# First batch of an attention kernel: scores by products of 64 rows, products with the values by 64 columns

## The chip, the core and the metric

The kernel runs on one NeuronCore of a Trainium2 chip. Its engines work side by side and wait for each other through semaphores: TensorE (PE) does matrix products and transposes, VectorE (DVE), ScalarE (ACT) and GpSimd (POOL) work element by element, SyncE (SP) issues most transfers. The metric is the device time of one execution in microseconds; lower is better.

## The reference

Three layers follow one another. Only the first is touched, and of it only the first of four batches.

```python
# q, k, v: 4 batches, 8 heads, 576 positions, head size 64
scores = scale * np.matmul(q, k.transpose(0, 1, 3, 2))
thresh = np.max(scores, axis=-1, keepdims=True) - tau
scores = np.where(scores >= thresh, scores, -1000000000.0)
attn = np.exp(scores - np.max(scores, axis=-1, keepdims=True))
attn = attn / (np.sum(attn, axis=-1, keepdims=True) + 1e-09)
x = np.matmul(attn, v)            # then 2304 tokens x 512
g = s * np.maximum(x @ w_in, 0) ** 2 + b
x = g @ w_out                     # d_ff 2048
h = x @ w_in2
out = (np.maximum(h, 0) + alpha * np.minimum(h, 0)) @ w_out2
```

## The kernel before

The instruction order is not written by hand. Every step is a task given to a planner (`Plan`, lines 114 to 216) with the engine that may do it, an assumed cost, the buffers it reads and writes, and a rank. `Plan.run` simulates the engines with these costs and emits, for each free engine, the ready task of lowest rank. A changed cost or a changed buffer thus changes the order of everything around it. `pe(n, k)` (line 244) is the assumed cost of `k` passes over `n` columns.

Attention works on pairs of heads: `pair(p)` (line 605), p = 0 to 3 for the first batch, 4 to 15 for the rest. A tile has 128 rows, so a pair's two heads of size 64 fill it. A pair has nine score tiles: four of each head (128 queries each) and one that holds the last 64 queries of both heads (`i == NQ`). The first batch is special (`first`, `whole`, `PLAIN`): its products are done in full f32, where each product appears in the trace as two weight loads and two matmul records. Later batches split every operand into a high and a low fp32r part (`hk`, `hq`, `gh`, `gl`) and are not touched here.

For a pair of the first batch:

- `transpose` (line 658, issued from line 660) turns k and q so that the head's dimensions lie on the rows. Evictions follow: L668 copies all 576 columns of k into `k32` in two instructions, and L676 (DVE) or L678 (ACT) writes q into `q32`, once for each head, multiplied by `sc_h[h]`, which holds the scale in that head's 64 rows and zero in the other 64.
- `score` (line 737, issued from L742) multiplies one 128x128 block of `q32` with `k32` in two products of 288 keys each, one for each half of the keys, into the two halves of a `sc` buffer. All 128 rows take part, the zeros in `q32` cancel the other head. There are two `sc` buffers.
- L752 (DVE) takes the negated maximum, L756 (ACT) the exponential, L758 (DVE) the threshold and the row sums. Each reads all of the `sc` buffer.
- `group` (line 838) turns a head's exponentials by 128 keys at a time (L877, and L881 for the shared tile), L887 (ACT) copies them into `gf` or `sh`, and `product` (line 845, issued from L852) multiplies them with the values. The weights of this product are `vt.t[:, c]`: the values of both heads, 128 columns, of which the 64 of the other head are of no use. 256 queries (`gi` 0) or 320 (`gi` 1) stream through; five products, one for each block of keys, add up in one bank. There are two heads and two `gi` for each pair: 16 groups, 80 products.
- `finish` (line 927) copies the bank into `z` (L934, ACT): for head 1 first over all 128 rows, then for head 0 over its 64 rows.

While this goes on, the planner fits in the preparation of the first weights (L351 to L411) and, once tokens and weights are there, the products of the second layer (L480 to L482, block A: the first 1536 tokens over part of the hidden size), whose rank is far behind all of attention. When all of attention is done, `switch` (line 1012) frees its memory and the rest of the two layers follows.

Of the kernel before, what the change touches and what calls it, by code (L numbers as in the profile page):

```python
# [12 lines left out]
AF = mybir.ActivationFunctionType  # L13
# [4 lines left out]
P = 128  # L18
# [201 lines left out]
def tile_kernel(ctx: ExitStack, tc: tile.TileContext, q, k, v, tau, w1i, w1o, s_in, b_in, w2i, w2o, alpha, out):  # L220
# [53 lines left out]
    def tiles(pool, n, name, shape, dt=F32):  # L274
        return [pool.tile(shape, dt, name=f"{name}{i}") for i in range(n)]
# [282 lines left out]
    def attention(ap):  # L558
# [26 lines left out]
        q32, k32 = tiles(ep, NP, "q32", [P, NS * P]), tiles(ep, NP, "k32", [P, S])  # L585
# [16 lines left out]
        def half(h):  # L602
            return (slice(0, D), slice(D, P)) if h == 0 else (slice(D, P), slice(0, D))

        def pair(p):
# [40 lines left out]
            for nm in "kq":  # L646
                t, hl = nat[nm], (ks if nm == "k" else qs)[0] if first else Buf(hk_s if nm == "k" else hq_s)
                qk[nm] = hl
                for tail in (False, True):
# [5 lines left out]
                    else:  # L655
                        tr = Buf(one_s, {"k": "misc", "q": "gt"}[nm]) if p == 0 and not tail else Buf(moe_s) if whole else Buf(one_s, "misc")
# [9 lines left out]
                    if first:  # L666
                        if nm == "k":
                            add("ACT", act(n), lambda hl=hl, tr=tr, c=c, n=n: nc.scalar.activation(  # L668
                                k32[p][:, c], tr.t[:, :n], AF.Copy), (tr,), (hl,), rank=ready)
                            continue  # L670
                        for h in range(2):
                            c0 = 2 * NQ * P + h * TL if tail else h * NQ * P

                            def scaled(e, h=h, c=slice(c0, c0 + n), tr=tr, of=cut_of):
                                if e == "DVE":
                                    nc.vector.tensor_scalar(q32[p][:, c], tr.t[:, of], sc_h[h], None, op0=ALU.mult)  # L676
                                else:
                                    nc.scalar.activation(q32[p][:, c], tr.t[:, of], AF.Copy, scale=sc_h[h])  # L678

                            add([("DVE", dve(n) + 0.065, ready), ("ACT", act(n, 1), ready)], 0, scaled, (tr,), (hl,))  # L680
                        continue
# [36 lines left out]
            for base, turns in stages:  # L718
                sums, rc, z = Buf(sums_s), Buf(rc_s), None
                es = {}  # L720
                for turn, i in enumerate(turns):
# [7 lines left out]
                    if first:  # L729
                        of, passes = (qs[0], ks[0]), [(q32[p], k32[p])]  # L730
# [6 lines left out]
                    def score(sp=sp, passes=passes, c=slice((col if first else ii) * P, ((col if first else ii) + 1) * P)):  # L737
# [586 lines left out]
```

## Time and profile before

| What | us |
|---|---|
| median of three runs | 1115.76 |
| lowest and highest | 1115.6, 1116.54 |
| profiled execution, span of its instructions | 1111.8 |
| median less that span | 3.96 |
| TensorE busy in the profiled execution | 1090.6 (98%) |
| VectorE busy | 911.6 (82%) |
| ScalarE busy | 755.5 (68%) |
| GpSimd busy | 352.1 (32%) |

The profile is one execution. A matmul record is longer than the time by which it delays the next one, since matmuls are pipelined: the cost of a matmul is read from the starts of consecutive records, not from their lengths. "PEld" is the weight load, which runs beside the matmul before it. A bracket behind a line of the timeline names an idle stretch and what ended it.

### The profile page before, as it was taken

To read this page: it belongs to the slowest core of one execution; us is meant where nothing else is said; L and a number is where in the kernel's file an instruction comes from. 1 tells how busy PE (TensorE), PEld (TensorE's weight loads), DVE (VectorE), ACT (ScalarE), POOL (GpSimd) and SP (SyncE) were. 2 spreads that over 40 slices of the span, in tenths; PEclk is the share of its full clock that TensorE was granted. 3 is DMA by queue.
4 is the path that set the end of the run, shared out by engine and by line. 5 is a ranking of instruction groups with operands and counts; after the bars stand their busy time and mean duration, and the time that the engine had idled before them with its cause. 6 is when DMAs were issued, how large, how long until landed. Compare 5 with 4: busy or idle time off the path is not lost.

```text
span 1111.8 us, 22073 instructions
## 1 busy us (share of the span) xinstructions
PE 1090.6 (98%) x7536; PEld 1051.7 (95%) x7536; DVE 911.6 (82%) x2055; ACT 755.5 (68%) x1737; POOL 352.1 (32%) x476
## 2 busy tenths in 40 slices
PE   8999999999999999999999999999999999999998
PEld 7777899998999999999999999999999999999998
DVE  4898888879888988757877789589986999998882
ACT  4888878867877868744554377357786998565551
POOL 1576764644654646500000013020120332112111
PEclk9999999999999999999999999999999999999999
DMA  5663363446444454044466565428834464554531
GB/s 119 177 167 123 107 168 86 109 118 156 109 118 118 118 124 108 12 139 134 125 217 209 173 205 161 126 86 278 279 132 164 146 211 154 159 160 119 154 90 39
DMA packets 185265, 158.36 MB, mean 142 GB/s; under 512 B 72000, under 2 KB 162112, under 8 KB 185152
## 3 DMA queue, kind: packets, MB, share of 16 engines
q1 hardware_dynamic: 182624, 154.79, 48.6%
q10 hardware_dynamic: 2528, 2.16, 0.7%
q8 instruction: 59, 0.97, 0.3%
q14 instruction: 54, 0.44, 0.1%
HBM read 91.10 MB, written 44.56 MB: 122 GB/s over the span
## 4 chain that ended last, share of the span: by engine, by line
PE 79%; DVE 9%; ACT 5%; DMA 3%; issue 2%; SPq 1%; POOL 0%; DVEq 0%; ACTq 0%; POOLq 0%
PE bank L480 12%; PE bank L481 11%; PE bank L482 11%; PE bank_b L481 8%; PE bank_b L480 8%; PE bank_b L482 8%; PE bank L852 7%; PE sc L742 7%; PE bank L877 5%; ACT e L756 1%; PE bank L881 1%; DVE e L758 1%; PE bank L660 1%; DMA stg<-wfi 1%; DVE mx L752 1%
## 5 line engine op out<-in xcount | busy, mean ns | idle before, releaser
L758 DVE SCALAR_TENSOR_TENSOR e<-sc,mx,e 128x576 f32<-128x576 f32 x144 | 116.3, 813 | 16.8 <-ACT e L756 13.2
L756 ACT ACTIVATE e<-sc,mx 128x576 f32<-128x576 f32 x144 | 106.4, 742 | 21.4 <-DVE mx L752 20.7
L877 PE MATMUL bank<-eyes,e 128*128 128x128 f32 (+1 forms) x640 | 120.2, 274 | 0.6 <-ACT gf L896 0.3
L752 DVE TENSOR_REDUCE mx<-sc 128x1 f32<-128x576 f32 x144 | 107.0, 751 | 13.7 <-PE sc L742 12.8
L877 PEld LDWEIGHTS bank<-eyes,e 128*128 128x128 f32 (+1 forms) x640 | 80.2, 139 | 13.4 <-issue 1.3
L480 PE MATMUL bank<-xt,wa 128*128 128x256 f32 (+1 forms) x266 | 84.3, 317 | 1.9 <-ACT rest L518 1.1
L480 PE MATMUL bank<-gt,wa 128*128 128x256 f32 (+1 forms) x267 | 83.5, 313 | 0.9 <-ACT rest L518 0.7
L481 PE MATMUL bank<-gt,wa 128*128 128x256 f32 (+1 forms) x267 | 78.9, 295 | 0.2 <-DVE gt L458 0.2
L482 PE MATMUL bank<-gt,wa 128*128 128x256 f32 (+1 forms) x267 | 78.9, 295 | 0.0
L754 POOL TENSOR_SCALAR mx<-mx,tau_s 128x1 f32<-128x1 f32 x144 | 51.4, 358 | 83.7 <-DVE mx L752 80.2
L482 PE MATMUL bank<-xt,wa 128*128 128x256 f32 (+1 forms) x266 | 76.8, 289 | 0.0
L481 PE MATMUL bank<-xt,wa 128*128 128x256 f32 (+1 forms) x266 | 76.7, 289 | 0.0
L742 PE MATMUL sc<-k,q 128*128 128x288 f32 x272 | 65.5, 369 | 1.8 <-DVE e L758 0.9
L852 PE MATMUL bank<-gl,vt 128*128 128x256 f32 (+1 forms) x192 | 64.8, 338 | 1.2 <-POOL gl L907 0.6
L852 PE MATMUL bank<-gh,vt 128*128 128x256 f32 (+1 forms) x192 | 57.8, 301 | 0.1
L541 ACT ACTIVATE gt<-rest,b_b,s_b 128x384 fp32r<-128x384 f32 x56 | 39.5, 708 | 26.5 <-DVE rest L539 26.3
L481 PE MATMUL bank_b<-gt,wa 128*128 128x384 f32 (+1 forms) x168 | 54.4, 324 | 1.1 <-DVE gt L531 1.0
L912 DVE TENSOR_TENSOR gl<-bank,gh 128x256 fp32r<-128x256 f32 (+1 forms) x96 | 43.4, 452 | 14.3 <-ACT gh L910 12.8
L480 PE MATMUL bank_b<-gt,wa 128*128 128x384 f32 (+1 forms) x168 | 54.3, 323 | 0.2 <-ACT n L1174 0.2
L480 PEld LDWEIGHTS bank<-xt,wa 128*128 128x128 f32 x266 | 50.4, 189 | 4.1 <-ACT rest L518 2.2
L482 PE MATMUL bank_b<-gt,wa 128*128 128x384 f32 (+1 forms) x168 | 54.1, 322 | 0.0
L922 POOL TENSOR_TENSOR gr<-gf,gh 64x256 fp32r<-64x256 f32 (+1 forms) x48 | 39.7, 828 | 44.2 <-DVE gl L920 43.0
(649 smaller groups left out, 4158.2 us busy)
## 6 DMA issues: line engine op xcount, KB each, us to landing
stg<-in_moe_w_in_dram SPq DMA_DIRECT2D x32, 512.0 KB, 4.0
stg<-in_moe_w_out_dram SPq DMA_DIRECT2D x32, 512.0 KB, 3.7
qo<-hq SPq DMA_DIRECT2D x32, 256.0 KB, 4.3
gf<-rest SPq DMA_DIRECT2D x30, 192.0 KB, 2.3
rest<-gf SPq DMA_DIRECT2D x40, 128.0 KB, 2.9
ko<-hk SPq DMA_DIRECT2D x32, 144.0 KB, 2.7
xr<-xs SPq DMA_DIRECT2D x6, 768.0 KB, 5.2
yf<-yb SPq DMA_DIRECT2D x24, 192.0 KB, 2.6
```

The lines of the kernel that those rows point to most:

```text
L480: nc.tensor.matmul(o, lhsT=wl, rhs=mh, start=first, stop=False, skip_group_check=on_top)
L481: nc.tensor.matmul(o, lhsT=wh, rhs=ml, start=False, stop=False, skip_group_check=on_top)
L482: nc.tensor.matmul(o, lhsT=wh, rhs=mh, start=False, stop=last, skip_group_check=on_top)
L742: nc.tensor.matmul(sp.t[:, x, :HS], lhsT=o[0][:, c], rhs=o[1][:, x * HS:(x + 1) * HS], start=n == 0, stop=n == len(passes) - 1)
L752: add("DVE", dve(S), lambda sp=sp, mx=mx: nc.vector.tensor_reduce(mx.t[:, 0:1], sp.t[:, :, :HS], op=ALU.max, axis=AX.XY, negate=True), (sp ...
L754: t2 = add("POOL", 0.26, lambda mx=mx: nc.gpsimd.tensor_scalar(mx.t[:, 1:2], mx.t[:, 0:1], -1.0, tau_s, op0=ALU.mult, op1=ALU.subtract), ( ...
L756: add("ACT", act(S, 1), lambda sp=sp, mx=mx, e=e: nc.scalar.activation(halves(e.t), sp.t[:, :, :HS], AF.Exp, bias=mx.t[:, 0:1]), (sp, mx), ...
L758: add("DVE", dve(S) + 0.065, lambda sp=sp, mx=mx, e=e, col=col, sums=sums: nc.vector.scalar_tensor_tensor(halves(e.t), sp.t[:, :, :HS], mx ...
L852: nc.tensor.matmul(o.t[:, :n], lhsT=w.rearrange("p a b -> p (a b)"), rhs=m.t[:, :n], start=c == first and x == 0, stop=c == last and x == ...
L877: nc.tensor.transpose(gt.t[:rows, m:m + P], es[i].t[:, keys], ident)
L912: add("DVE", dve(n), lambda hi=hi, lo=lo, gt=gt: nc.vector.tensor_tensor(lo.t[:, :n], gt.t[:, :n], f32(hi.t[:, :n]), op=ALU.subtract), (gt ...
L922: add("POOL", pool2(n), lambda hi=hi, f=f, hf=hf: nc.gpsimd.tensor_tensor(hi.t[:TL, :n], f.t[:TL, :n], f32(hf.t[:TL, :n]), op=ALU.subtract ...
```

## The change

- `q32` and `k32` become pairs of planes. Plane 0 of `k32` holds the first half of the keys, plane 1 the second half with its two heads' rows exchanged; both planes of `q32` hold the queries, plane 1 again with the rows exchanged. The keys' order becomes: two blocks of 128, the 64 tail keys, two blocks of 128 (the `keys` slices follow it).
- A new function `twice` evicts the transposes into them: 13 instructions a pair where there were 6 (three of k's and three of q's main columns, three and four of the tails). Each may run on ACT or DVE.
- The score of a one-head tile becomes two products of 64 rows instead of 128: the first half of the keys in the head's own rows, the second half in the other 64 rows. The shared tile still takes 128 rows, with zeros in the unused places (one more GpSimd memset for each of four `q32` tiles).
- A product with the values becomes two products: the 64 columns of this head's values as weights, half of the queries each, one into rows 0 to 63 of the bank, one into rows 64 to 127.
- `finish` copies twice half of the columns, all to the head's own rows.
- The assumed costs of both kinds of task are lowered: `pe(HS, 8)` to `pe(HS, 4) + 0.1`, and `pe(n, 4)` to `pe(n, 2) + 0.1`.

```diff
-        q32, k32 = tiles(ep, NP, "q32", [P, NS * P]), tiles(ep, NP, "k32", [P, S])
+        q32, k32 = tiles(ep, NP, "q32", [P, 2, NK * P]), tiles(ep, NP, "k32", [P, 2, HS])
+        for t in q32:
+            nc.gpsimd.memset(t[:, :, NQ * P:], 0.0)
...
+        def twice(p, nat, q_of, k_of, rank):
+            n = HS - G1
+            tk, tq, tt = (Buf(one_s, "misc"), Buf(one_s, "gt"), Buf(moe_s)) if p == 0 else (Buf(moe_s), Buf(moe_s), Buf(moe_s))
...
+                w = cols.stop - cols.start
+                add([("ACT", act(w, by is not None), rank), ("DVE", dve(w) + 0.065 * (by is not None), rank)], 0, go, (tr,), (to,))
+            every, (lo, hi) = slice(0, P), half(0)
+            add("PE", pe(P, NQ), lambda: turned(nat["k"], tk, range(NQ)), (nat["k"],), (tk, k_of), rank=rank)
+            add("PE", pe(P, NQ), lambda: turned(nat["q"], tq, range(NQ)), (nat["q"],), (tq, q_of), rank=rank)
+            move((q32[p][:, 0, :NQ * P], every), tq, slice(0, NQ * P), q_of, sc_p)
+            move((k32[p][:, 0, :G1], every), tk, slice(0, G1), k_of)
+            for a, b in (lo, hi), (hi, lo):
+                move((k32[p][a, 1, n:], b), tk, slice(G1, 2 * G1), k_of)
+            add("PE", pe(P), lambda: turned(nat["k"], tt, (NQ,)), (nat["k"],), (tt, k_of, q_of), rank=rank)
+            move((k32[p][:, 0, G1:], every), tt, slice(0, n), k_of)
+            for a, b in (lo, hi), (hi, lo):
+                move((k32[p][a, 1, :n], b), tt, slice(n, 2 * n), k_of)
+            for a, b in (lo, hi), (hi, lo):
+                move((q32[p][a, 1, :NQ * P], b), tq, slice(0, NQ * P), q_of, sc_p)
+            for h, b in enumerate((lo, hi)):
+                for x, a in enumerate((b, (hi, lo)[h])):
+                    move((q32[p][a, x, NQ * P + h * TL:NQ * P + (h + 1) * TL], b), tt, slice(TL, P), q_of, sc_p)
...
+                    def by_keys(sp=sp, h=h, c=slice(ii * P, (ii + 1) * P)):
+                        for x in range(2):
+                            r = slice(0, P) if h is None else half(h ^ x)[0]
+                            nc.tensor.matmul(sp.t[:, x, :HS], lhsT=q32[p][r, x, c], rhs=k32[p][r, x], start=True, stop=True)
...
-                    add("PE", pe(HS, 8) if first else pe_r(HS, 2 * len(passes)), score, of, (sp,), rank=rank - AHEAD)
+                    add("PE", (pe(HS, 8) if h is None else pe(HS, 4) + 0.1) if first else pe_r(HS, 2 * len(passes)), by_keys if first else score, of, (sp,), rank=rank - AHEAD)
...
+                    if plain:
+                        for r, x in (half(0)[0], slice(0, n // 2)), (half(1)[0], slice(n // 2, n)):
+                            nc.tensor.matmul(
+                                o.t[r, :n // 2], lhsT=vt.t[:, c, h], rhs=mv[0].t[:, x], start=c == first, stop=c == last)
+                        return
...
-                t = add("PE", pe(n, 4) if plain else pe_r(n, len(mv)), go, (vt, *mv), (o,), after=(chain if plain else prods)[-1:], rank=rank)
+                t = add("PE", pe(n, 2) + 0.1 if plain else pe_r(n, len(mv)), go, (vt, *mv), (o,), after=(chain if plain else prods)[-1:], rank=rank)
...
-                outs[1, gi] = add("ACT", act(n), lambda: nc.scalar.activation(
-                    z.t[r, c], ob.t[r, :n], AF.Copy), (ob,), (z,), after, rank)
+                for i in range(2):
+                    x = slice(c.start + i * n // 2, c.start + (i + 1) * n // 2)
+                    outs[1, gi] = add("ACT", act(n // 2), lambda x=x, i=i: nc.scalar.activation(
+                        z.t[a, x], ob.t[half(i)[0], :n // 2], AF.Copy), (ob,), (z,), (), rank)
```

## Rows read from the trace of the kernel before

**Rows 1.** The page: busy us, share and instructions by engine.

```profile
PE 1090.6 (98%) x7536; PEld 1051.7 (95%) x7536; DVE 911.6 (82%) x2055; ACT 755.5 (68%) x1737; POOL 352.1 (32%) x476
```

**Rows 2.** Windows: stretch, length, then busy us of PE, PEld, DVE, ACT, POOL; clock, DMA.

```profile
10.00:30.00 20.00, 19.25 (x97) 15.27 (x97) 10.79 (x25) 10.34 (x25) 2.15 (x7) 1.00 0.62 126
30.00:80.00 50.00, 48.17 (x255) 36.55 (x254) 44.96 (x100) 43.64 (x102) 32.85 (x40) 1.00 0.66 180
80.00:131.00 51.00, 50.74 (x294) 40.73 (x294) 45.93 (x96) 43.40 (x91) 35.14 (x39) 1.00 0.34 107
131.00:200.00 69.00, 68.07 (x555) 66.90 (x554) 58.79 (x136) 54.87 (x124) 41.55 (x61) 1.00 0.53 131
200.00:300.00 100.00, 96.18 (x762) 92.35 (x761) 83.91 (x203) 77.86 (x177) 53.46 (x79) 1.00 0.50 121
300.00:400.00 100.00, 98.11 (x793) 95.88 (x791) 88.50 (x208) 76.59 (x176) 56.38 (x81) 1.00 0.46 118
400.00:478.00 78.00, 76.99 (x627) 75.41 (x626) 62.13 (x147) 57.72 (x133) 41.95 (x64) 1.00 0.31 76
478.00:1111.00 633.00, 625.89 (x4141) 622.02 (x4139) 514.36 (x1138) 388.39 (x909) 85.82 (x93) 1.00 0.52 160
```

**Rows 3.** Waits of PE, DVE and ACT, 20 to 130 us: total, times, longest.

```profile
PE bank L852 <- ACT sh L887: 0.8, 3, 0.3
...
DVE mx L752 <- PE sc L742: 4.5, 11, 0.9
ACT gf L887 <- PE bank L877: 3.2, 3, 1.7
ACT z L934 <- PE bank L852: 2.0, 4, 0.9
```

**Rows 4.** Timeline of PE, 40 to 47 us: start, length, instructions, idle before.

```profile
40.38 0.60 PE L852 MATMUL bank<-gf,v 128*128 128x256 f32 x2
40.82 0.38 PE L877 MATMUL bank<-eyes,e 128*64 128x128 f32 x2
41.04 1.14 PE L742 MATMUL sc<-k,q 128*128 128x288 f32 x4
42.01 0.59 PE L852 MATMUL bank<-sh,v 128*128 128x256 f32 x2
42.44 0.38 PE L811 MATMUL bank<-eyes,rb 128*128 128x128 f32 x2
42.66 0.60 PE L852 MATMUL bank<-gf,v 128*128 128x256 f32 x2
...
45.57 0.70 PE L852 MATMUL bank<-sh,v 128*128 128x256 f32 x2 [0.26 <-ACT sh L887]
46.11 0.38 PE L877 MATMUL bank<-eyes,e 128*128 128x128 f32 x2
```

**Rows 5.** Timeline of PE, 113 to 114 us: a product with 320 queries.

```profile
113.04 0.70 PE L852 MATMUL bank<-gf,v 128*128 128x320 f32 x2
113.58 0.38 PE L877 MATMUL bank<-eyes,e 128*64 128x128 f32 x2
```

**Rows 6.** The instructions of L852: count, min/median/max ns, first and last start us.

```profile
L852 PE MATMUL bank<-gf,v x96: 379/432/537, 19.3 to 131.2; 128*128 128x256 f32 x48, 128*128 128x320 f32 x48
L852 PE MATMUL bank<-sh,v x64: 379/432/537, 20.0 to 130.4; 128*128 128x256 f32 x32, 128*128 128x320 f32 x32
```

**Rows 7.** Groups by line and shape, 0 to 131 us: busy us, mean ns, idle before.

```profile
L887 ACT ACTIVATE gf<-bank 128x320 f32<-128x320 f32 x16 | 7.0, 435 | 0.6 <-PE bank L881 0.6
L887 ACT ACTIVATE gf<-bank 128x256 f32<-128x256 f32 x16 | 6.2, 387 | 3.2 <-PE bank L877 3.2
L887 ACT ACTIVATE gf<-bank 64x320 f32<-64x320 f32 x8 | 3.4, 426 | 1.6 <-PE bank L881 1.6
L676 DVE TENSOR_SCALAR q<-bank,by_half 128x512 f32<-128x512 f32 x4 | 3.0, 750 | 3.9 <-PE bank L660 3.1 <-ACT q L678 0.7
L678 ACT ACTIVATE q<-bank,by_half 128x64 f32<-128x64 f32 x4 | 1.1, 313 | 1.4 <-DVE q L676 1.4
L668 ACT ACTIVATE k<-bank 128x64 f32<-128x64 f32 x4 | 0.9, 224 | 1.1 <-PE bank L660 1.0
```

**Rows 8.** The instructions of L676: count, min/median/max ns, first and last start us.

```profile
L676 DVE TENSOR_SCALAR q<-bank,by_half x8: 274/516/751, 7.6 to 40.5; 128x512 f32<-128x512 f32 x4, 128x64 f32<-128x64 f32 x4
```

**Rows 9.** Timeline, 7 to 10 us: the evictions ahead of the first score.

```profile
7.56 0.75 DVE L676 TENSOR_SCALAR q<-bank,by_half 128x512 f32<-128x512 f32 x1 [3.09 <-PE bank L660]
8.35 0.69 ACT L678 ACTIVATE q<-bank,by_half 128x512 f32<-128x512 f32 x1 [6.34 <-DVE q L676]
8.93 0.92 ACT L668 ACTIVATE k<-bank 128x512 f32<-128x512 f32 x2
9.05 0.47 DVE L676 TENSOR_SCALAR q<-bank,by_half 128x64 f32<-128x64 f32 x2 [0.74 <-PE bank L660]
9.57 4.21 PE L742 MATMUL sc<-k,q 128*128 128x288 f32 x8 [0.56 <-ACT k L668]
```

More of the change, by code (lines that the diff above doesn't have):

```diff
@@ L603, in half, with turned, move, go @@
             return (slice(0, D), slice(D, P)) if h == 0 else (slice(D, P), slice(0, D))
+        def twice(p, nat, q_of, k_of, rank):
+            n = HS - G1
+            tk, tq, tt = (Buf(one_s, "misc"), Buf(one_s, "gt"), Buf(moe_s)) if p == 0 else (Buf(moe_s), Buf(moe_s), Buf(moe_s))
+            def turned(t, tr, cs):
+                for i, c in enumerate(cs):
+                    nc.tensor.transpose(tr.t[:, i * P:(i + 1) * P], t.t[:, c].rearrange("p h d -> p (h d)"), ident)
+            def move(o, tr, cols, to, by=None, rows=P):
+                def go(e, o=o):
+                    d, r = o
+                    if by is None:
+                        if e == "DVE":
+                            nc.vector.tensor_copy(d, tr.t[r, cols])
+                        else:
+                            nc.scalar.activation(d, tr.t[r, cols], AF.Copy)
+                    elif e == "DVE":
+                        nc.vector.tensor_scalar(d, tr.t[r, cols], by[r], None, op0=ALU.mult)
+                    else:
+                        nc.scalar.activation(d, tr.t[r, cols], AF.Copy, scale=by[r])
+                w = cols.stop - cols.start
[16 more added lines that the diff above has]
+                    move((q32[p][a, x, NQ * P + h * TL:NQ * P + (h + 1) * TL], b), tt, slice(TL, P), q_of, sc_p)
@@ L645, in pair @@
             qk, ends = {}, ((sc_h[0], slice(NQ * P, S)), (sc_h[1], slice(S, S + TL)))
-            for nm in "kq":
-                t, hl = nat[nm], (ks if nm == "k" else qs)[0] if first else Buf(hk_s if nm == "k" else hq_s)
+            if first:
+                twice(p, nat, qs[0], ks[0], ready)
+            for nm in () if first else "kq":
+                t, hl = nat[nm], Buf(hk_s if nm == "k" else hq_s)
                 qk[nm] = hl
@@ L655, in pair @@
                     else:
-                        tr = Buf(one_s, {"k": "misc", "q": "gt"}[nm]) if p == 0 and not tail else Buf(moe_s) if whole else Buf(one_s, "misc")
+                        tr = Buf(one_s, "misc")
                         def transpose(t=t, tr=tr, cs=(NQ,) if tail else tuple(range(NQ))):
@@ L665, in pair @@
                     cut_of = slice(s0, s0 + n)
[L666 to L681, printed above, removed]
                     if nm == "k":
@@ L729, in pair @@
                     if first:
[L730 removed]
+                        of, passes = (qs[0], ks[0]), ()
                     elif h is None:
```

9 lines of the change are left out of this document (6 added, 3 removed).

## The prediction

> **What bounds the kernel now.** I first read the page's busy shares [rows 1]: PE 98%, the next engine 82%. That alone says little, since a matmul record is longer than what it costs, so I went to the windows [rows 2]. The change touches what runs from about 10 to 131 us, the first batch's attention. There PE is busy for 19.25 of 20, 48.17 of 50 and 50.74 of 51 us, at a granted clock of 1.00. DVE needs 10.79, 44.96 and 45.93, ACT 10.34, 43.64 and 43.40: half idle at the start, then some 90% and 86%. From 131 us to the end of attention at about 478 us PE stays between 96% and 99%, DVE at 80 to 89%, ACT at 74 to 80%; behind that it is PE again (625.89 of 633). So PE sets the end throughout, but in the stretch of the change two other engines stand close behind it. The waits say the same [rows 3]: in 20 to 130 us the largest wait of DVE that PE ends is 4.5 us in total, that of ACT 3.2, while PE's own largest is 0.8.
>
> What a product costs on PE I read from starts in the timeline [rows 4]. A score starts at 41.04 and the next instruction at 42.01: 0.97 us for four records, 0.2425 each. A product with the values of 256 queries runs from 40.38 to 40.82 or from 42.01 to 42.44: 0.43 us, two records of 0.216. One of 320 queries takes 113.04 to 113.58, 0.54 us [rows 5]. There are 160 records of such products, 80 products, the last started at 131.2 us [rows 6]; the scores of one head are 8 in each of four pairs, 32. Together that is 32 x 0.97 + 40 x 0.43 + 40 x 0.54 = 31.0 + 17.2 + 21.6 = 69.8 us of PE in a stretch of 121 us: a large lever.
>
> **The change part by part.**
>
> *Scores.* A one-head score keeps two products of 288 columns, four records, four weight loads. Only if records of different row halves run at the same time is anything saved. The two records of one product use the same rows, so they must follow each other, and I expect the order of the program to hold: first A1, A2 on one row half, then B1, B2 on the other. Then only B1 can run beside A2, and three record times remain of four. Saved: one record, 0.2425 us a score, 32 x 0.2425 = 7.8 us. No row of this trace shows two matmuls at once, so the bounds are far apart: nothing saved, or both products wholly side by side, 32 x 0.485 = 15.5 us. I take the middle, since every record of [rows 4] starts behind the one before it.
>
> *Products with the values.* Each becomes four records of half the columns, with weight loads of 64 columns. By the same order three quarters remain: 0.108 us saved at 256 queries, 0.135 at 320, 40 x 0.243 = 9.7 us. Bounds: 0 and 19.4 us. Gross on PE: 17.5 us, between 0 and 35.
>
> *Entering and leaving the smaller shapes.* Nearly every score and product stands between transposes of the full shape [rows 4], so 32 + 80 = 112 visits make some 224 changes of shape. Their price is the largest unknown. From below: the transposes with 64 weight columns ("128*64") take 40.82 to 41.04, 0.22 us for two, as much as two of full width at 42.44 to 42.66, so 64 columns alone cost nothing to enter or leave. A gain on top is excluded, as full-shape neighbours already follow each other without a gap. From above: if the array must run empty, a start costs what it costs after a wait: the product at 45.57 takes 0.54 us to the next start where others take 0.43, 0.11 more; 224 x 0.11 = 24.6 us. I take a quarter, 6.2 us, nearer to the row that shows a change of shape, though it is one of columns only. Net on PE: 17.5 - 6.2 = 11.3 us.
>
> [...]
>
> [...]
>
> *Evictions (`twice`).* Before, a pair has six: for q 0.75 on DVE and 0.69 on ACT, for k 0.60 and 0.22, for the tails 0.31 and 0.28, together 2.9 us. After, there are thirteen. Rows do not shorten an instruction (64x320 takes 426 ns, 128x320 takes 435 [rows 7]), columns do. So three of 512 scaled columns are 3 x 0.72, three of 256 are 3 x 0.39, three of 32 about 3 x 0.22, four of 64 about 4 x 0.3: 5.2 us. That is 2.3 us more a pair, shared by DVE and ACT. For pair 0 nothing covers it: the first score starts at 9.57, released by the last eviction of k, while DVE and ACT had begun at 7.56 [rows 9]. Two engines share 2.3 us, so everything starts 1.2 us later; all of that counts. For pairs 1 to 3 it is 6.9 us of engine time, prepared ahead of use and done by about 41 us (the last of L676 starts at 40.5 [rows 8]), much of it while DVE and ACT are half idle; it costs nothing unless that idle time is gone, at most 3.5 us (half of 6.9).
>
> *`finish`.* 16 instructions become 32 of half the columns: 2 x 0.28 against 0.39, 2 x 0.31 against 0.44, the halves read between 224 ns at 64 columns and 387 at 256 [rows 7]. That adds about 0.18 us each, 2.8 us of ACT. ACT has 14% idle from 30 us on, which covers it; uncovered, it is the bank of the products that is held 0.18 us longer, and the next group waits for that bank: at most 2.8 us. The four memsets on GpSimd come ahead of its first work on a score, and it is busy for 2.15 of the 20 us from 10 us on [rows 2]: they delay nobody.
>
> *The planner's costs.* Cheaper PE tasks let the planner bring tasks from behind forward. No transfer is moved as such; the SP queue keeps its loads, whose ranks are unchanged.
>
> **From PE to the end.** In 10 to 131 us DVE works 101.7 us and ACT 97.4; with the additions (9.7 us, half each) DVE stands at about 106. If the stretch shrank by all of 11.3 us to 110, DVE would have to be 97% busy, which no window shows; 90% and 92% is the most so far. What helps is that PE can take products of the second layer into its free time and that DVE has 15% left behind 131 us (58.79 of 69). I let three quarters through: 8.5 us. Sum: -8.5 + 1.2 = -7.3 us. The profiled execution would go from a span of 1111.8 to 1104.5; the median stands 3.96 us above the span, so 1115.8 becomes **1108.5 us**.
>
> **The rivals.**
>
> *Whole overlap.* Both halves run side by side in full: gross 35 us, less 6.2, three quarters of 28.8 is 21.6, less 1.2: about 1095; with the price of a visit at 0.1 us and two half-length products as the planner assumes, 32 x 0.38 + 40 x 0.12 + 40 x 0.17 = 23.8, three quarters less 1.2: 1099. For it: nothing in a product of one half needs the other. Against it: the order of the records.
>
> *Swallowed.* PE gains as forecast, but DVE and ACT, 90% busy, set the pace: only a quarter, 2.8 us, comes through, less 1.2: 1114. For it: the windows from 30 to 131 us. Against: DVE and ACT wait longer for PE (4.5 and 3.2 us) than PE for them (the largest is 0.8) [rows 3].
>
> *No overlap.* The change does not do what it says: f32 records of two halves follow each other as before. No gain, 1.2 us later at the start, up to 4.9 us (half of 9.7) where the added DVE and ACT work is uncovered: 1117 to 1122.
>
> *Drains.* Each change of shape empties the array, at 0.11 us: 24.6 us against a gross of 17.5, PE needs 7.1 us more, all of it on the bound, plus 1.2: 1124. Without overlap it is 24.6 + 1.2, 1141. It decides from 17.5 / 112 = 0.156 us a visit on: above that the kernel is slower. For it: full shapes stand on both sides of almost every visit. Against: the 64-column transposes.
>
> **How the numbers follow.** Forecast 0.36 (own range 1103 to 1112), whole overlap 0.17, swallowed 0.18, no overlap 0.14, drains 0.15. About 0.2%, 2.2 us, is what a measurement of this kernel can tell from no change. Faster by more than that: forecast, whole overlap and 0.04 of swallowed, 0.57. Within it: the rest of swallowed and 0.05 of no overlap, 0.19. Slower: 0.24. For 8 in 10 the range reaches down to 1097, which leaves out the lower end of whole overlap, and up to 1121, which leaves out most of the drains.
>
> **What would show it.** In the changed profile a score of one head should take about 0.73 us from its first start to the next instruction's (0.97: no overlap; 0.49 to 0.59: whole overlap), a product of 256 queries about 0.32 and one of 320 about 0.40, plus up to 0.06 for a change of shape. The shared tile's score stays at 0.97. The first score should start near 10.8 us, the first batch end near 123 instead of 131 us, and PE stay at 96% or more from 30 us on; idle PE behind evictions of ACT or maxima of DVE would mean swallowed. A start-to-start time of the transposes behind a product far above 0.11 us would mean drains, and the forecast would be wrong by its largest term.

## The result and the profile after

The changed kernel takes 1129.1 us (median, 1127.1 to 1130.5) beside 1115.7 for the kernel before: a ratio of 1.0119 with an interval of 1.0105 to 1.0133. It is 13.4 us **slower**; the forecast was 7.3 us faster. The profiled execution took 1127.07 us, its span 1125.3.

Page of the changed kernel, busy us, share and instructions (answers to [rows 1]):

```profile
PE 1087.5 (97%) x7696; PEld 1025.6 (91%) x7696; DVE 928.3 (82%) x2087; ACT 756.5 (67%) x1751; POOL 348.5 (31%) x478
```

Windows of the changed kernel, columns as in [rows 2]:

```profile
10.00:30.00 20.00, 17.26 (x120) 9.93 (x118) 15.31 (x39) 13.54 (x33) 2.13 (x7) 1.00 0.61 123
30.00:80.00 50.00, 44.29 (x318) 23.28 (x318) 44.27 (x102) 45.10 (x108) 28.28 (x36) 1.00 0.66 174
80.00:131.00 51.00, 50.02 (x371) 32.76 (x368) 38.82 (x82) 43.19 (x96) 33.16 (x39) 1.00 0.30 93
131.00:200.00 69.00, 59.22 (x457) 56.66 (x457) 61.04 (x126) 47.13 (x106) 33.51 (x44) 0.93 0.52 128
200.00:300.00 100.00, 96.34 (x754) 91.63 (x754) 85.95 (x205) 74.43 (x170) 55.89 (x81) 1.00 0.47 115
300.00:400.00 100.00, 98.45 (x796) 96.23 (x795) 81.47 (x189) 74.04 (x167) 59.43 (x85) 1.00 0.43 104
```

PE works 3.1 us less than before and is idle for 37.8 us of its span instead of 21.2. Of these 16.6 us two stretches hold 14.7. From 10 to 80 us (5.9 us) PE is no longer full: 17.26 of 20 and 44.29 of 50 us, where it was 19.25 and 48.17; from 30 to 80 us DVE and ACT are as busy as PE. From 131 to 200 us (8.9 us) PE works 59.22 us instead of 68.07, and the mean clock is 0.93. In the first stretch PE's largest waits, from 10 to 80 us (total, times, longest), are for an eviction of q and for the copies behind the transposes:

```profile
PE bank L614 <- ACT q L627: 2.0, 3, 1.4
PE bank L887 <- ACT gf L930: 2.0, 4, 0.9
```

The second is mostly one stall. Windows of 5 us, then one beside it from the kernel before, then waits of PE and ACT from 140 to 160 us, then the instructions of L410, which prepares the first weights, after and before (count, min/median/max ns, first to last start):

```profile
145.00:150.00 5.00, 2.65 (x20) 2.19 (x19) 4.67 (x10) 3.78 (x12) 3.99 (x5) 1.00 0.92 229
150.00:155.00 5.00, 0.63 (x6) 0.43 (x4) 5.00 (x9) 1.81 (x5) 3.40 (x4) 0.61 0.82 178
155.00:160.00 5.00, 4.11 (x19) 4.14 (x20) 5.00 (x9) 2.00 (x5) 2.11 (x2) 0.50 0.91 191
```

```profile
150.00:155.00 5.00, 5.00 (x41) 5.00 (x42) 4.75 (x14) 3.83 (x10) 4.89 (x7) 1.00 0.86 199
```

```profile
PE bank L892 <- DMA vt<-vt: 5.3, 1, 5.3
ACT wa L410 <- POOL n L406: 3.7, 2, 3.2
PE sc L777 <- DVE e L793: 1.9, 1, 1.9
```

```profile
L410 ACT ACTIVATE wa<-n x20: 613/626/685, 41.4 to 153.9; 128x512 fp32r<-128x512 f32 x20
L410 ACT ACTIVATE wa<-n x20: 617/630/668, 37.5 to 132.6; 128x512 fp32r<-128x512 f32 x20
```

TensorE waits 5.3 us for the values of a later pair, a copy that GpSimd's work at L741 comes ahead of. The second layer's products, which fill such pauses elsewhere, need the first weights, and these are prepared until 153.9 us; in the kernel before the last of the 20 started at 132.6. That earlier weights would have filled this pause is argued, not shown. The granted clock is 1.00 until 151 us, 0.50 from 152 to 161 us and 1.00 again from 162 us on: it falls behind a window in which PE was busy for 2.65 of 5 us, at the start of the long wait. At 0.50 two transposes of L920 take 0.43 us from their start to the next instruction's (159.01 to 159.44), at 1.00 they take 0.22 (163.24 to 163.46).

The small shapes themselves, timeline of PE (answers to [rows 4]):

```profile
42.35 0.44 PE L887 MATMUL bank<-gf,v 128*64 128x128 f32 x4 [0.93 <-ACT gf L930]
42.72 0.44 PE L920 MATMUL bank<-eyes,e 128*128 128x128 f32 x2
43.09 0.44 PE L887 MATMUL bank<-sh,v 128*64 128x128 f32 x4
43.46 0.76 PE L770 MATMUL sc<-k,q 64*128 64x288 f32 x4
44.30 0.44 PE L887 MATMUL bank<-gf,v 128*64 128x128 f32 x4
```

```profile
98.27 0.29 PE L482 MATMUL bank<-xt,wa 128*128 128x256 f32 x1
98.49 0.76 PE L770 MATMUL sc<-k,q 64*128 64x288 f32 x4
99.17 0.38 PE L480 MATMUL bank<-xt,wa 128*128 128x256 f32 x1
```

A product takes 0.37 us from its start to the next (0.43 before), but the two transposes between it and the next small product take 0.37 instead of 0.22 us. By the starts of their records 0.06 of that falls on the first, behind the product, and 0.09 on the second, ahead of the next one. So 0.06 is won and 0.15 lost, +0.09. A score takes 0.69 us to the next instruction (98.49 to 99.17; the 0.84 from 43.46 to 44.30 has a short wait in it). With 0.09 ahead and 0.06 behind, as at the transposes, that is 0.84 instead of 0.97 us, -0.13. This holds for a visit that stands alone. Where a score and a product follow each other, no full shape stands between them that would take the 0.06 and 0.09 us longer (the product at 43.09 takes the same 0.37 us to the score behind it), so I count 0.15 us saved, an estimate: in the changed kernel's trace the 112 scores and products stand in 89 visits.

### The profile page after: what moved, and what is told of

It is laid out like the page before. It is cut to its first block, busy times and chain, and to the rows that moved or that the text cites. A ratio compares the mean times of both kernels' runs of the same rounds, so it can differ in the third digit from the quotient of the medians.

```text
span 1125.3 us, 22455 instructions
## 1 busy us (share of the span) xinstructions
PE 1087.5 (97%) x7696; PEld 1025.6 (91%) x7696; DVE 928.3 (82%) x2087; ACT 756.5 (67%) x1751; POOL 348.5 (31%) x478
## 4 chain that ended last, share of the span: by engine, by line
PE 78%; DVE 9%; ACT 6%; DMA 3%; issue 2%; POOL 1%; SPq 1%; DVEq 0%; ACTq 0%; POOLq 0%
PE bank L480 11%; PE bank L481 11%; PE bank L482 11%; PE bank_b L481 8%; PE bank_b L480 8%; PE bank_b L482 8%; PE bank L920 5%; PE sc L777 5%; PE bank L892 4%; PE bank L887 2%; PE bank L924 1%; PE sc L770 1%; ACT e L791 1%; DVE mx L787 1%; DVE e L793 1%
## 5 line engine op out<-in xcount | busy, mean ns | idle before, releaser
L920 PE MATMUL bank<-eyes,e 128*128 128x128 f32 (+1 forms) x640 | 124.8, 280 | 1.5 <-DVE e L793 0.8
L791 ACT ACTIVATE e<-sc,mx 128x576 f32<-128x576 f32 x144 | 106.1, 741 | 14.7 <-DVE mx L787 14.0
L480 PE MATMUL bank<-gt,wa 128*128 128x256 f32 (+1 forms) x350 | 109.5, 313 | 1.8 <-ACT rest L518 1.7
L481 PE MATMUL bank<-gt,wa 128*128 128x256 f32 (+1 forms) x350 | 105.0, 300 | 0.6 <-DVE gt L531 0.3
L482 PE MATMUL bank<-gt,wa 128*128 128x256 f32 (+1 forms) x350 | 104.8, 300 | 0.0
L920 PEld LDWEIGHTS bank<-eyes,e 128*128 128x128 f32 (+1 forms) x640 | 75.6, 139 | 19.2 <-issue 11.0
L789 POOL TENSOR_SCALAR mx<-mx,tau_s 128x1 f32<-128x1 f32 x144 | 47.4, 330 | 99.5 <-DVE mx L787 86.5
L480 PEld LDWEIGHTS bank<-gt,wa 128*128 128x128 f32 x350 | 66.6, 190 | 3.4 <-ACT rest L518 2.3
L481 PEld LDWEIGHTS bank<-gt,wa 128*128 128x128 f32 x350 | 66.6, 190 | 1.0 <-DVE gt L531 0.5
L482 PEld LDWEIGHTS bank<-gt,wa 128*128 128x128 f32 x350 | 66.5, 190 | 0.0
L538 ACT ACTIVATE rest<-bank_b 128x384 f32<-128x384 f32 x42 | 20.5, 489 | 48.8 <-PE bank_b L482 48.7
```

The source lines that it names most:

```text
L480: nc.tensor.matmul(o, lhsT=wl, rhs=mh, start=first, stop=False, skip_group_check=on_top)
L481: nc.tensor.matmul(o, lhsT=wh, rhs=ml, start=False, stop=False, skip_group_check=on_top)
L482: nc.tensor.matmul(o, lhsT=wh, rhs=mh, start=False, stop=last, skip_group_check=on_top)
L789: t2 = add("POOL", 0.26, lambda mx=mx: nc.gpsimd.tensor_scalar(mx.t[:, 1:2], mx.t[:, 0:1], -1.0, tau_s, op0=ALU.mult, op1=ALU.subtract), ( ...
L791: add("ACT", act(S, 1), lambda sp=sp, mx=mx, e=e: nc.scalar.activation(halves(e.t), sp.t[:, :, :HS], AF.Exp, bias=mx.t[:, 0:1]), (sp, mx), ...
L920: nc.tensor.transpose(gt.t[:rows, m:m + P], es[i].t[:, keys], ident)
```

## The experiments

All ratios are to the kernel before, run beside it on the same chip.

**The told costs.** The diff also lowers what the planner, which writes the order of all engines, is told of these products: 0.59 for a score and 0.32 and 0.37 for the products, where the chip shows about 0.84, 0.52 and 0.57.

```diff
 # e1: the changed kernel, told what the chip shows
-    pe(HS, 4) + 0.1        # scores
+    pe(HS, 4) + 0.35
-    pe(n, 2) + 0.1         # products
+    pe(n, 2) + 0.3
 # e2: the changed kernel, told the old costs
+    pe(HS, 8)
+    pe(n, 4)
 # e3: the kernel before, told the low costs; nothing else
-    pe(HS, 8)
+    pe(HS, 4) + 0.1
-    pe(n, 4)
+    pe(n, 2) + 0.1
```

> The changed kernel with the planner's assumed costs raised to what its trace shows: a score of 64 rows takes 0.09 us before its first record, 0.69 to the next instruction and 0.06 more on that one, 0.84 together (assumed was 0.59), a product with the values 0.52 (256 queries) and 0.57 (320) where 0.32 and 0.37 were assumed. Theory P (the order, planned with costs that are 24 us too low in sum, is what loses the time): back near the kernel before, -4 to +4 us against it. Theory C (the smaller shapes and the added evictions cost the time themselves): stays +10 to +15 us.

Measured: 1125.97 us, 1.0101 (1.0073 to 1.0129). Told about what the chip shows, the planner still ends some 11 us late, so it is not only that the told costs were too low.

> The changed kernel with the assumed costs of the kernel before (0.98 for a score, 0.44 and 0.54 for the products), so that the plan is close to the old one and errs to the high side. Theory P: within 4 us of the kernel before. Theory C: +10 to +15 us.

Measured: 1121.78 us, 1.0055 (1.0040 to 1.0070). No stall at 145 us.

> The kernel before with nothing but the lowered assumed costs (0.59 for a score of one head, 0.32 and 0.37 for the products); its instructions are the old ones, which take 0.97, 0.43 and 0.54. The assumption is then 32 x 0.38 + 40 x 0.11 + 40 x 0.17 = 23 us too low, about as much as in the changed kernel. Theory P: +10 to +16 us, with PE idle around 140 to 160 us. Theory C: within 2 us of the kernel before.

Measured: 1129.26 us, 1.0128 (1.0108 to 1.0148). The kernel before, with every instruction as it was, loses 14 us when the planner is told less, and it has the changed kernel's stall. So the low told costs are enough for the whole loss; in the changed kernel itself taking them back (e2) returns some 7 of the 13 us. Windows of e3, and a wait of PE from 140 to 160 us:

```profile
150.00:155.00 5.00, 0.42 (x4) 0.22 (x2) 3.84 (x7) 2.24 (x4) 4.28 (x4) 0.69 0.62 142
155.00:160.00 5.00, 4.02 (x19) 4.02 (x20) 0.93 (x1) 0.00 (x0) 3.71 (x4) 0.50 1.01 218
```

```profile
PE bank L480 <- DVE wa L411: 5.6, 1, 5.6
```

Here PE waits for the first weights themselves (L411), prepared until 153.9 us as in the changed kernel.

**Parts of the change.**

```diff
 # e4: the changed kernel with products and finish as before; a score told 0.84
 # e5: the kernel before with products and finish of the change, told 0.52 and 0.57
 # e7, e8, e9: e2 (one order) with the old shapes again
-    r = slice(0, P) if h is None else half(h ^ x)[0]
+    r = slice(0, P)                      # e7, e9: 128 rows, both heads summed
-    for r, x in (half(0)[0], ...), (half(1)[0], ...): matmul(o.t[r, :n // 2], ...)
+    matmul(o.t[:, :n], ...)              # e8, e9: 128 columns
 # e10: e4 with 128 rows (both heads summed) and the old told cost: the 13 evictions alone
```

> Only the scores changed (64 rows, both planes, 13 evictions a pair), products with the values and their copies as before, assumed costs as measured (0.84 and the old ones). PE should need 32 x 0.13 = 4.2 us less than before. Theory P: -4 to +1 us against the kernel before. Theory C, if the evictions are what costs: +5 us or more.

Measured: 1118.6 us, 1.0026 (1.0015 to 1.0037).

> The kernel before with the products alone by 64 columns and the finish in two copies; the scores and the evictions are those of before, and the planner is told 0.3 us more than the columns take (0.52 for the product of 256 columns, close to what the changed kernel's trace shows). Theory V (a visit to the small shapes costs about 0.31 us, whatever the planner thinks): 64 products of 256 columns become 0.09 longer and 16 of 320 0.035 longer, that is 6.3 us more of TensorE for at least the 64 and up to 6 us more of ScalarE for the second copies, which are beside other work: +3 to +7 us, 1118.5 to 1123. Rival of the prediction (a visit costs 0.055 us): 9.7 us of products saved less 4.4 of changes, -5 us, 1110.5. Rival O (only the order that the planner makes decides): within +-3 us, of either sign.

(That expectation, like those of e15 and e17, counts 64 and 16 products; [rows 6] has 40 and 40, which makes 4.8 us of TensorE instead of 6.3.) Measured: 1123.71 us, 1.0080 (1.0067 to 1.0093), more than either count gives.

> As the run with the old assumed costs, in exactly its order, but every score takes all 128 rows (part of the computation changed: it then sums both heads). Theory S (TensorE's cost of the smaller shapes counts): a score takes 0.97 instead of 0.84, so 3 to 4 us slower than that run, about +10 against the kernel before. Theory E (the added evictions and copies make up the +6): within 1.5 us of that run, +5 to +7.

> As the run with the old assumed costs, in its order, but the products with the values take all 128 columns of the values and all queries at once, as before the change (the copies behind them still read two halves, part of the computation changed). Theory S: products take 0.43 and 0.54 instead of 0.52 and 0.57, 5 us of TensorE less, so about +1 to +3 against the kernel before. Theory E: +5 to +7.

> As the run with the old assumed costs, in its order, with scores and products both in the full shape (part of the computation changed as in the two others). What then differs from the kernel before is the evictions (13 for 6), the two copies for one in finish, the memsets, and the order they lead to. Theory E: +5 to +7 against the kernel before. Theory S: by TensorE's sums (scores cost 4 us more, products 5 us less than in the smaller shapes) the same +5 to +7 minus 1 us if only work counts, but 0 to +3 if the smaller shapes also cost a lower clock or waits.

Measured: e7 1.0073 (1.0055 to 1.0091), e8 1.0063 (1.0048 to 1.0078), e9 1.0060 (1.0045 to 1.0075), beside 1.0055 for e2. In one order, old or new shapes make no difference that can be measured.

> The changed kernel's second copies of queries and keys (13 evictions for 6) with everything else as before: scores by whole products of 128 rows (which sum both heads, so the scores are other numbers), products whole, one finish copy, the old assumed costs. Theory E (the evictions at the start are not covered: ScalarE and VectorE set the pace of the first 60 us): +3 to +5 us, 1118.5 to 1121. The prediction's step (the evictions of pairs 1 to 3 cost nothing, pair 0 costs 1.2): 1116.5 to 1117.5. If this is within 1 us of before, the 6.5 us left with the old costs come from products and finish.

Measured: 1128.72 us, 1.0128 (1.0114 to 1.0142). The evictions alone, planned anew, cost as much as the whole change, though e4, which has them too, costs 2.9 us. Windows of e10:

```profile
10.00:30.00 20.00, 16.84 (x94) 13.48 (x95) 13.29 (x31) 12.04 (x30) 2.07 (x7) 1.00 0.60 120
30.00:80.00 50.00, 43.62 (x220) 32.05 (x219) 45.34 (x98) 44.08 (x100) 27.34 (x35) 1.00 0.53 152
```

PE is short of work in the same stretch as in the changed kernel, at full clock and with the old shapes.

**How much of TensorE's time reaches the end, and the price of a visit.**

```diff
 # e12: e2, each score of one head issued twice
-    for x in range(2):
+    for x in (0, 1) if h is None else (0, 1, 0, 1):
```

> The changed kernel with the old assumed costs, each of the 32 scores of one head issued twice into the same bank, one straight behind the other (the second writes the same numbers again); nothing else changed, and the planner is told nothing of it. It prices what a score costs inside a visit. Whole overlap with a price a visit: the second issue costs its streaming alone, 0.49 us, 32 x 0.49 = +15.5 us over the same kernel with single issues (1121.8 against 1115.2), 1135 to 1139. A price at each matmul (no overlap, or the loads unhidden each time): 0.84 x 32 = +27, 1146 to 1150. No overlap at all and no price: 0.97 x 32 = +31, 1151 to 1154. In the trace: from a score's first record to the next operation 0.686 us becomes about 1.2 under the first, 1.4 under the second.

Measured: 1125.85 us, 1.0100 (1.0086 to 1.0114). Timeline of PE:

```profile
44.93 1.24 PE L770 MATMUL sc<-k,q 64*128 64x288 f32 x8
46.10 0.44 PE L887 MATMUL bank<-gf,v 128*64 128x128 f32 x4
```

Eight records take 1.17 us, four 0.69: a second score in the same visit costs 0.48 us, half of 0.97, so the two halves overlap wholly and the rest is a price of the visit. But 32 x 0.48 = 15.4 us more of TensorE moved the end by 0.45% beside e2, 5 us: a third, and by the two intervals between a sixth and a half.

**The stall.**

```diff
 # e6, e13: the changed kernel; due times of the first weights
-W1I = 50, 30
-W1O = 200, 15
+W1I = 20, 20       # e6        -200, 10   # e13
+W1O = 120, 12      # e6        -100, 10   # e13
```

> The changed kernel with its low assumed costs, but with the preparation of the first weights ranked earlier (ranks 20 + 20u and 120 + 12u instead of 50 + 30u and 200 + 15u). Theory W (the low costs hurt because the weights come 27 us later, the second layer's products starve at 145 to 160 us and TensorE falls to its lower clock level): the stall goes and the time returns to about +4 to +8 us against the kernel before, where the old costs stood (+6). Theory O (the order of attention itself is what suffers): stays at +11 to +15.

Measured: 1133.82 us, 1.0160 (1.0145 to 1.0175). It did not test what it was meant to: L410 still ran to 157.5 us.

> The changed kernel with the first weights' preparation ranked ahead of the attention (due -200 and -100 with a step of 10, for 50 and 200 with steps of 30 and 15): all its tasks stand earlier in the engines' orders. Theory W (the low assumed costs let attention tasks push the weights' preparation back, and TensorE then stands idle at 145 to 156 us and falls to half clock, some 7 us in all): no stall at 140 to 160 us, clock full there; the weights' engine time at the start then delays the first batch by what their tasks take on ScalarE and GpSimd ahead of it, so the time gets better by less than 7 us: 1121 to 1127. Rival O (it is not this stall but the attention's order over the whole of the 480 us): stall gone, time unchanged or slower, 1128 to 1136.

Measured: 1131.61 us, 1.0154 (1.0139 to 1.0170). L410 and two windows of it:

```profile
L410 ACT ACTIVATE wa<-n x20: 612/630/677, 13.0 to 113.1; 128x512 fp32r<-128x512 f32 x20
```

```profile
10.00:30.00 20.00, 13.90 (x80) 9.15 (x78) 14.08 (x29) 15.00 (x33) 7.97 (x9) 1.00 0.87 219
155.00:160.00 5.00, 4.82 (x39) 4.48 (x37) 4.57 (x14) 4.18 (x11) 3.62 (x5) 1.00 0.27 63
```

The weights come 41 us earlier and the clock stays full at 150 to 160 us, but PE is now idle at the start (13.90 of 20 us), and the time is no better. So the stall is where the changed kernel's loss shows, not a cost that could be taken out by itself.

**The old order held fast.** The next three keep every task and every told cost of the kernel before, so that all engines run in its order (in the traces PE, DVE, ACT and POOL pass through the same tiles in the same sequence); only the instructions inside a task differ. The two behind them keep the instructions and change only told costs.

```diff
 # e14: before, scores by halves inside the old task (a score sums half of its rows)
+    r = half(x)[0] if first and h is not None else slice(0, P)
-    lhsT=o[0][:, c], rhs=o[1][:, x * HS:(x + 1) * HS]
+    lhsT=o[0][r, c], rhs=o[1][r, x * HS:(x + 1) * HS]
 # e15: before, products by 64 columns, one finish copy, which reads one half twice; e16: e14 and e15
 # e17: before, told 0.13 less a score, 0.09 and 0.035 more a product
 # e18: before, told 0.01 more a product
-    pe(n, 4)
+    pe(n, 4) + 0.01
```

> The kernel before with every task in its old order and with its old assumed cost; the 32 scores of one head in the first batch are products of rows 0 to 63 for the first half of the keys and of rows 64 to 127 for the second (so they take only half of what they should sum, and the numbers are others). Theory S (shapes count, by the visit price read from the traces: 0.84 for 0.97 us): 32 x 0.13 = 4.2 us of TensorE less, of which a third to all reaches the end (doubling 32 scores moved the end by 5 of 15.5 us): -1.4 to -4.2 us, 1110.5 to 1113. The prediction's price (0.055 a visit, three quarters overlap): 7.8 - 1.8 = 6.0 us of TensorE less, three quarters through: 1110. Rival (a tile of 64 rows costs more than the trace shows, the old order fits the old durations): 1115 to 1119.

> The kernel before with every task in its old order and with its old assumed cost; the first batch's products with the values are made by 64 columns, halves of the queries (one finish copy reads the upper half twice, so the output is another there). Theory S: 64 x 0.09 + 16 x 0.035 = 6.3 us of TensorE more, a third to all of it at the end: +2 to +6 us, 1116.5 to 1121. The prediction's price: 9.7 - 4.4 = 5.3 us less, three quarters through: 1110.5. Theory O says of it: within 1.5 us of before, since the order is that of before, and the +9 us of the run of the products alone came from the new order.

> Both of these together in the old order (with both, scores and output are other numbers). Theory S: -4.2 + 6.3 = +2.1 us of TensorE, +0.7 to +2.1 at the end: 1115 to 1117. The prediction's price: 11.3 us of TensorE less, three quarters through: 1106. If it is above 1119, the shapes explain a good part of the changed kernel's time by themselves, and theory O loses its share.

Measured: e14 0.9996 (0.9984 to 1.0007), e15 1.0002 (0.9993 to 1.0011), e16 1111.50 us, 0.9975 (0.9964 to 0.9987). **The shapes do not make the kernel slower**; together they win 2.8 us. Windows of e16:

```profile
30.00:80.00 50.00, 45.43 (x330) 24.52 (x328) 45.35 (x101) 44.39 (x104) 33.66 (x40) 1.00 0.67 181
131.00:200.00 69.00, 67.97 (x550) 66.26 (x550) 58.17 (x138) 54.97 (x125) 42.20 (x62) 1.00 0.54 132
```

In 30 to 80 us PE is busy for 45.43 us instead of 48.17 and the stretch is over hardly sooner (the 24th maximum starts at 80.5 us instead of 81.1): there PE waits away most of what it wins. The rest of the gain comes by the end of the first batch: its last product starts at 128.8 us instead of 131.2. Behind that all is as before.

e14's gain is partly hidden. Windows of e14, with a line of VectorE's timeline and a wait of PE from 20 to 40 us:

```profile
25.00:30.00 5.00, 1.49 (x9) 0.63 (x7) 0.87 (x4) 0.33 (x2) 0.00 (x0) 0.85 0.49 44
30.00:35.00 5.00, 4.74 (x20) 3.66 (x21) 3.95 (x9) 3.46 (x8) 0.29 (x1) 0.50 1.14 319
```

```profile
29.50 0.17 DVE L979 TENSOR_SCALAR nal_b<-nal_b 128x16 f32<-128x16 f32 x1 [3.99 <-DMA nal_b<-in_moe_alpha_dram]
PE bank L660 <- ACT q L678: 3.8, 1, 3.8
```

In the order of before VectorE has to wait for the load of a small constant of the last layer, 4.0 us here and 1.1 before; an eviction of q stands behind it and PE behind that (3.8 us), and the granted clock falls (0.85, then 0.50). e14's two executions with a granted clock of 1.000 took 1111.8 and 1112.7 us, its ten at 0.996 to 0.998 took 1112.9 to 1117.0.

> The kernel before, all its work as it was; only the planner is told other durations: 0.13 us less for each of 32 scores, 0.09 more for 64 products and 0.035 more for 16 (what the small shapes really take). Theory O (any new order costs): +3 to +12 us, 1118 to 1127. Theory S or E: within 1.5 us of before, 1113 to 1116.5. Told too low by 24 us in sum the same kernel took 14 us more with a stall of TensorE at 145 to 160 us; here the sum told is 2 us higher, so that stall should be absent.

> The kernel before, all its work as it was, with one number changed: the planner is told 0.01 us more for each product of the first batch (0.44 for 0.43). Theory O: the new order costs +2 to +10 us though no duration differs, 1117 to 1125. Otherwise within 1.5 us of before. The first batch's middle maxima, which set the pace of TensorE at 30 to 60 us, come later in it under theory O.

Measured: e17 1117.55 us, 1.0028 (1.0019 to 1.0036); e18 1117.0 us, 1.0017 (1.0008 to 1.0026). No instruction differs from before; the order alone costs 3.1 and 1.9 us. A part of that goes with the clock: e18's four executions at a granted clock of 0.999 took 1114.8 to 1117.0 us, its three at 0.996 took 1118.4 to 1118.7.

```diff
 # e19: the whole change in the old order
 # each old eviction's task holds the new ones that replace it (3, 3; 1, 2, 2, 2); finish: both copies
-    add("ACT", act(n), lambda ...: nc.scalar.activation(k32[p][:, c], ...), (tr,), (hl,), rank=ready)
+    add("ACT", act(n), moved, (tr,), (hl,), rank=ready)     # moved: three copies; cut short
```

> The whole change in the order of before: each old eviction's place in the engines' orders holds the new evictions that stand for it (3 for each of the keys' two, 1, 2, 2 and 2 for the queries' four), the finish's place holds both copies, and every assumed cost is the old one. Theory O (the new order is what costs): the shapes' -2.8 us and the engine time of 7 evictions a pair and 16 second copies, partly covered, +0.5 to +4: 1112 to 1116, not slower than before. Theory E (evictions and copies are not covered): +3 to +7 over the run with both shapes in the old order, 1115 to 1119. If above 1119, both are wrong and something else in the change costs.

Measured: 1126.15 us (1119.8 to 1132.2), 1.0095 (1.0066 to 1.0124). Against e16 this adds 28 evictions, 16 copies and four memsets in the old order, and it costs 1.2%, some 13 us. It is harsher than the change in one way: all evictions of the keys stay on ScalarE, where the changed kernel gives some to VectorE. Windows of e19:

```profile
30.00:35.00 5.00, 2.56 (x19) 1.98 (x20) 3.58 (x7) 4.25 (x10) 0.29 (x1) 1.00 1.01 288
35.00:40.00 5.00, 4.57 (x38) 2.45 (x38) 4.96 (x11) 4.15 (x14) 3.52 (x3) 1.00 0.51 136
40.00:45.00 5.00, 2.85 (x20) 1.51 (x18) 2.35 (x6) 4.90 (x13) 3.06 (x5) 0.89 0.66 178
45.00:50.00 5.00, 5.00 (x24) 2.15 (x22) 4.06 (x8) 3.46 (x9) 1.69 (x3) 0.50 0.23 51
65.00:70.00 5.00, 5.00 (x23) 2.54 (x22) 3.02 (x9) 3.02 (x7) 1.04 (x2) 0.50 0.31 106
```

PE is idle for 2.4 and 2.2 us of the first and third window, ACT is busy there (4.25 and 4.90 of 5), and then the clock is at half until past 70 us. From 10 to 16 us it is at half too. Without these evictions (e16) the granted clock is 1.00 throughout 15 to 131 us. No run separates the engine time from the clock that falls behind it, but by an estimate from the windows the clock is a large part: PE is busy for some 32 us at 0.50, work of 16 us at full clock by the two transposes of the changed kernel (0.43 and 0.22 us), and this execution (1129.81 us) is 18 us longer than e16's median. The six executions differ: the one with the highest granted clock, 0.997, took 1119.8 us, the two with the lowest, 0.984 and 0.988, 1129.8 and 1132.2.

**Summed up.** Work of before or of the change, by told costs of before or of the change:

| | old told costs | low told costs |
|---|---|---|
| work of before | 1 | 1.0128 (e3) |
| work of the change | 1.0055 (e2) | 1.0119 |

Either alone makes the kernel slower, and they don't add up: with the low costs the work makes no difference that these runs can tell. Each of the four has an order of its own.

## Why the prediction was wrong

**The step that failed is "The planner's costs".** I saw that cheaper tasks let others be brought forward, named no price, and went on to the queues. That one edit, alone, costs 14 us (e3). Told costs even 0.01 us off cost 1.9 (e18), and costs near the truth still 11 (e1): what was missing is the order as such, not only its false costs. Most other unseen costs were bounded from both sides; the order was not, and no rival was made of it. Nor was a fall of the clock behind new idle time, which put TensorE at half clock (0.50) for 10 us in the changed kernel.

**Evictions.** "It costs nothing unless that idle time is gone, at most 3.5 us" failed as well. The engine time was sized about right: summed over their records, the 52 evictions of the changed kernel take 20.2 us of DVE and ACT where the 24 before take 11.5, 8.8 us more (the step had 4 x 2.3), and the finish copies 9.1 instead of 6.5 (2.6 more, the step had 2.8). What counted was where it stands. In [rows 2] ACT and DVE were 87 to 90% busy from 30 to 80 us, and I priced their added work as throughput. Each eviction is a link in the chain from transpose to score, maximum, exponential and product. In one order the additions to ScalarE and VectorE cost some 13 us, with the clock that falls behind them (e19 against e16); planned anew, between 2.9 (e4, with the scores) and 14.2 us (e10). For pair 0 the step had the wrong sign in the changed kernel: the first score starts at 8.83 us, not at 10.8 (9.57 before), since a score now begins with the half of the keys that VectorE copies first. In the old order (e19) it starts at 10.5.

**Order of the records.** Wrong: the four records come in two pairs. A product's start at 43.088, 43.094, 43.248 and 43.255 us. The trace doesn't name the halves; the reading that fits is A1 and B1 together, then A2 and B2, wholly side by side. So the gross gain is the upper bound, 35 us, not 17.5.

**Entering and leaving.** That a visit costs time was right, the size was not: alone, scores win 32 x 0.13 = 4.2 us and products lose 40 x 0.09 + 40 x 0.03 = 4.8. So 112 visits that stand alone would eat all 35 us, 0.32 us a visit; the 23 that are shared give back some 3.5 us (23 x 0.15, an estimate). I took 0.055, and even the upper bound was 0.22 (two changes at 0.11). For one change of shape that bound was about right: 0.09 us on the instruction ahead, and a score's last pair of records takes 0.33 us to the next instruction instead of 0.24. What the term left out is the rest: the first records of a score are 0.35 us apart instead of 0.24, and a transpose behind takes 0.06 longer. The weight loads fit that: the first load of the score at 98.49 us and that of the instruction behind it start with their matmuls (PEld 98.48 and 99.17, PE 98.49 and 99.17), where in the kernel before the load of the score at 41.04 starts at 40.93, 0.11 us ahead. No run tests whether this makes the price, and none shows whether the array runs empty at a change of shape, as the upper bound supposed.

**From PE to the end.** Three quarters were to come through. A third did in e12, where PE had idle time already, and about half in the old order: in e16 PE is busy for 1084.6 us of a span of 1108.8, where it was 1090.6 of 1111.8, 6.0 us less for 3.0. From 30 to 80 us "swallowed", with its 90% busy DVE and ACT, was the better reading of [rows 2]: in e16 PE's busy time there falls and the stretch stays almost as long. The waits of [rows 3] misled: PE waited for little because it could take second-layer work, and that shows nothing of what a shorter score is worth.

**The rivals.** "Drains" gave 1124, on the right side, by a price for the change of shape. The trace shows one (0.15 us for two transposes between small products), but in the old order the smaller shapes cost nothing in sum (e16: 2.8 us faster), and that the array empties was not shown. Its number was near the result for another reason. The 1129.1 us lies outside the range of 1097 to 1121.

**Still open.** e16 wins 2.8 us, and e14 and e15 win nothing singly. Shared visits and e14's clock go far to explain it: in e16 112 scores and products stand in 85 visits, which makes PE's sum -4.2 + 4.8 - 27 x 0.15, some -3.5 us (an estimate), and e14's two executions at full clock stand some 2.4 us below the kernel before. Why e15's 4.8 us do not show is open. Nor was it settled why the planner's new orders end 2 to 14 us later, beyond the places shown. Of the kernels that do the whole work none was faster than the kernel before.

## What to carry to other kernels

Where a planner orders the engines by told costs, price the order as an unknown with both signs, and test a change of shape with the order held fast before judging it: here the order moved the time by up to 14 us, the shapes by 3. Small products that stood alone among full ones here paid some 0.32 us a visit, so try to group several in one visit; a second score in a visit cost 0.48 us, half of a full one. A part of a small saving or loss can be the clock, so compare the granted clock of the executions too (e14, e18, e19). Before calling an engine the bound of a stretch, ask what share of a saving there would arrive: doubling one of its operations is a run that tells.

## What the runs showed of the hardware

Products in f32 on two row halves, or two column halves, start in pairs 6 to 7 ns apart in the changed kernel; for two row halves a second score in the same visit costs 0.48 us, half of the 0.97 of a full one (e12), so these overlap in full. Between such a product and a full shape time is lost on both sides: 0.09 us on the instruction ahead and 0.06 on a transpose behind, 0.15 us for two transposes between two of them (0.37 instead of 0.22).

And in several traces idle time of TensorE was followed by a lower clock. The granted clock fell to 0.50 in the changed kernel behind 5 us with 2.65 us of work, at the start of a wait of 5.3 us; in e3 behind 5 us with 3.15 and 1.8 us with 0.42; in e14 within a window with 1.49; in e19 within one with 2.85, behind windows with 2.56 and 4.57. It stayed there for about 10 us in the first two, 7 in e14 and 27 in e19. In e16 it stayed at 1.00 through a window with 2.97 of 5 us (25 to 30 us).

In the kernel before it is 1.00 in every window of [rows 2], but the first of them hides something: its first two scores take 4.21 us for eight records [rows 9], about twice 8 x 0.2425. Four transposes that start at 13.57 us take 0.85 us to the next instruction, four at 14.42 take 0.44. So a matmul took about twice its later time until some 14 us there, and a part of PE's 19.25 of 20 us in that window is work at that pace.
